# A layer norm + linear attention + gelu MLP block on one core: stages over all tokens instead of an interleaved schedule

## The chip, the cores and the metric

One core of a Trainium2 chip. The metric is the device time of one execution in microseconds (us); smaller is better. Most executions agree within about 1.5%. Now and then one execution has a much lower granted TensorE clock (0.757 in a run of 331.8 us for the kernel before); such slow runs are listed apart and no reading below uses them. PE is TensorE, DVE is VectorE, ACT is ScalarE, POOL is GpSimd.

## The reference, cut to what matters

```python
# x: (1, 2048, 640)   32 heads of width 20   hidden width F = 1536   all bf16
xn = layernorm(x)
q, k, v = split_heads(xn @ wqkv)                # three (2048, 640) matrices
phi(t)  = where(t > 0, t + 1, exp(t)) + 1e-6
kv  = sum over tokens of phi(k)^T v             # per head, 20x20
z   = sum over tokens of phi(k)                 # per head, 20
o   = (phi(q) @ kv) / (phi(q) @ z + 1e-6)       # per head
mlp = gelu_tanh(xn @ w1 + b1) @ w2 + b2
return x + o @ wo + mlp
```

## The kernel before

It works in two parts. First, token tile by token tile (16 tiles of 128), it normalises, transposes, computes K and V together and adds phi(K)^T V into PSUM. Then, in four chunks of 512 tokens, it interleaves Q, the MLP's hidden blocks ("h"), the attention division and the output products. The hidden block:

```python
def h_head(c, jb):                                      # one block: 128 hidden columns x 512 tokens
    # ... 5 matmuls of 512 columns into H_ps[s2]
    act(hsh, H_ps, Identity, bias=b1h, scale=0.5)       # ScalarE
    act(sq,  H_ps, Square,   bias=b1h, scale=0.5)       # ScalarE
    dve.tensor_scalar(vv, sq, C1x4, C0, mult, add)      # VectorE
    dve.tensor_tensor(uu, vv, hsh, mult)                # VectorE
    # later units:
    act(th, uu, Tanh, scale=2.0)                        # ScalarE, same table as Exp
    dve.scalar_tensor_tensor(GT, th, 1.0, hsh, add, mult)
# ... (cut)
def g_units(c):                                         # the interleaved order
    us = []
    for t in range(DT):                                 # DT = 5
        us += [("qt", c, t), ("h", c, t), ("h", c, t + DT)]
    us += [("den", c), ("h", c, 2 * DT), ("h", c, 2 * DT + 1), ("rdenT", c)]
    return us
# ... (cut) output: W2 (12 blocks) and Wo (5 blocks) as 512+128 columns per token tile
```

Of the kernel before, what the change touches and what calls it, by code (L numbers as in the profile page):

```python
# [5 lines left out]
ALU = AluOpType  # L6
ACT = mybir.ActivationFunctionType
P = 128
# [104 lines left out]
def bass_parallel_sum__linear_attn_block__dense_activation_gelu__prompt_kernel(  # L113
# [3 lines left out]
    assert Batch == 1 and D % P == 0 and F % P == 0 and S % 512 == 0  # L117
# [8 lines left out]
    assert DH * H == D  # L126
# [4 lines left out]

    with contextlib.ExitStack() as es:
        sb = lambda *a, **k: es.enter_context(nc.sbuf_tensor(*a, **k))

        x_res = sb("x_res", [P, NT, D], BF16)
        xnT = sb("xnT", [P, DT, S], BF16)
        Wkv = sb("Wkv", [P, DT, 2 * D], BF16)
        Wq = sb("Wq", [P, DT, D], BF16)
        W1 = sb("W1", [P, DT, F], BF16)
        Wo = sb("Wo", [P, DT, D], BF16)  # L140
        W2 = sb("W2", [P, JT, D], BF16)
        b1tmp = sb("b1tmp", [JT, P], BF16)
        b1h = sb("b1h", [P, JT], FP32)
        b2bc = sb("b2bc", [P, D], BF16)
        ones_row = sb("ones_row", [1, P], BF16)
        ones_col = sb("ones_col", [P, 1], BF16)
        ident = sb("ident", [P, P], BF16)
        stats = sb("stats", [P, 3, 12], FP32)
        aggr = sb("aggr", [P, 3, 2], FP32)
        rstd = sb("rstd", [P, 3], FP32)  # L150
        nmr = sb("nmr", [P, 3], FP32)
        veps = sb("veps", [P, 3], FP32)
        epscol = sb("epscol", [P, 1], FP32)
        mhalf = sb("mhalf", [P, 1], FP32)
        xn_tm = sb("xn_tm", [P, 2, D], BF16)
        ek = sb("ek", [P, 2, D], BF16)
        rk = sb("rk", [P, 2, D], BF16)
        PK = sb("PK", [P, 2, D], BF16)
        Vaug = sb("Vaug", [P, 2, D + DT], BF16)

        e0 = [DH * ((P * dt) // DH) for dt in range(DT)]
        e1 = [DH * (-((-(P * (dt + 1))) // DH)) for dt in range(DT)]
        Wd = [e1[dt] - e0[dt] for dt in range(DT)]
        voff = []
        acc = 0
        for dt in range(DT):
            voff.append(acc)
            acc += Wd[dt] + 1
        VAW = acc
        Vaug = sb("Vaug2", [P, 2, VAW], BF16)  # L170
        maskKV = [sb(f"maskKV{dt}", [P, Wd[dt]], BF16) for dt in range(DT)]
        mt_lo = [e0[dt] // P for dt in range(DT)]
        mt_hi = [(e1[dt] - 1) // P for dt in range(DT)]
        kvw_base = [mt_lo[dt] * P for dt in range(DT)]
        kvw_w = [(mt_hi[dt] - mt_lo[dt] + 1) * P for dt in range(DT)]
        KVW = [sb(f"KVW{dt}", [P, kvw_w[dt]], BF16) for dt in range(DT)]
        pairs = [[dt for dt in range(DT) if mt_lo[dt] <= mt <= mt_hi[dt]] for mt in range(DT)]
        EB = sb("EB", [P, DT, H], BF16)
        ZB = sb("ZB", [P, DT, H], BF16)
        z_sb = sb("z_sb", [P, DT], FP32)  # L180
        E32 = sb("E32", [H, D], BF16)
        PQT = sb("PQT", [P, 2, DT, CW], BF16)
        eqb = sb("eqb", [P, 4, CW], BF16)
        rq = sb("rq", [P, 4, CW], BF16)
        den_sb = sb("den_sb", [P, CH, H], FP32)
        rden = sb("rden", [P, CH, H], BF16)
        rdenT = sb("rdenT", [H, CW], BF16)
        numsb = sb("numsb", [P, 4, CW], BF16)
        OT = sb("OT", [P, 2, DT, CW], BF16)
        hsh = sb("hsh", [P, 4, CW], BF16)  # L190
        sq = sb("sq", [P, 4, CW], BF16)
        vv = sb("vv", [P, 4, CW], BF16)
        uu = sb("uu", [P, 4, CW], BF16)
        th = sb("th", [P, 4, CW], BF16)
        GT = sb("GT", [P, 2, JT, CW], BF16)
        out_sb = sb("out_sb", [P, 2, D], BF16)

        ps = es.enter_context(nc.psum_tensor("ps", [P, 8 * 512], FP32))

# [3 lines left out]
        def bankbf(b, lo=0, hi=1024):  # L203
            return ps[:, b * 512:(b + 1) * 512].bitcast(BF16)[:, lo:hi]

        psT = [bankbf(6, 0, DT * P), bankbf(7, 0, DT * P)]
        K_A = bank(2, 0, 512)
        K_B = bank(3, 0, D - 512)
        K_full = ps[:, 2 * 512: 2 * 512 + D]
        V_A = bank(4, 0, 512)  # L210
        V_B = bank(5, 0, D - 512)
        V_full = ps[:, 4 * 512: 4 * 512 + D]
        KVB0, KVB1 = 0, 1
        kvb = {}
        order6 = [0, 1, 3]
        order7 = [2, 4]
        off = 0
        for dt in order6:
            kvb[dt] = (KVB0, off)
            off += Wd[dt] + 1  # L220
        assert off <= 512
        off = 0
        for dt in order7:
            kvb[dt] = (KVB1, off)
            off += Wd[dt] + 1
        assert off <= 512

        def kv_block(dt, extra=True):
            b, o = kvb[dt]
            return bank(b, o, o + Wd[dt] + (1 if extra else 0))  # L230

        b1T_ps = bankbf(2, 0, JT)

        qT_ps = [bank(4), bank(5)]
        H_ps = [bank(6), bank(7)]
        NUM_ps = [bank(0), bank(2)]
        R_ps = [bank(1), bank(3)]
        NUM_psl = [bank(4), bank(6)]
        R_psl = [bank(5), bank(7)]
        FA = [bank(0), bank(2)]  # L240
        FB = [bank(1, 0, D - 512), bank(3, 0, D - 512)]
        F_full = [ps[:, 0:D], ps[:, 2 * 512: 2 * 512 + D]]

        r_x = [R_("x%d" % c) for c in range(NC)]
        r_xnT = [R_("xnT%d" % t) for t in range(NT)]
        r_Wkv, r_Wq, r_W1, r_Wo, r_W2 = R_("Wkv"), R_("Wq"), R_("W1"), R_("Wo"), R_("W2")
        r_b1tmp, r_b1h, r_b2bc = R_("b1tmp"), R_("b1h"), R_("b2bc")
        r_xt = [R_("xt%d" % t) for t in range(NT)]
        r_identc = R_("identc")
        r_csmall = R_("csmall")  # L250
        r_mask = R_("mask")
        r_EB, r_E32 = R_("EB"), R_("E32")
        r_stats = [R_("stats%d" % i) for i in range(3)]
        r_aggr = [R_("aggr%d" % i) for i in range(3)]
        r_rstd = [R_("rstd%d" % i) for i in range(3)]
        r_nmr = [R_("nmr%d" % i) for i in range(3)]
        r_veps = [R_("veps%d" % i) for i in range(3)]
        r_xn = [R_("xn0"), R_("xn1")]
        B_ = [R_("bank%d" % i) for i in range(8)]
        r_psT = [[B_[6]], [B_[7]]]  # L260
        r_K, r_V = [B_[2], B_[3]], [B_[4], B_[5]]
        r_ek = [R_("ek0"), R_("ek1")]
        r_rk = [R_("rk0"), R_("rk1")]
        r_PK = [R_("PK0"), R_("PK1")]
        r_Va = [R_("Va0"), R_("Va1")]
        r_KV = [B_[0], B_[1]]
        r_KVW = R_("KVW")
        r_zsb, r_ZB = R_("zsb"), R_("ZB")
        r_b1T = [B_[2]]
        r_qT = [[B_[4]], [B_[5]]]  # L270
        r_eq = [R_("eq%d" % i) for i in range(4)]
        r_rq = [R_("rq%d" % i) for i in range(4)]
        r_PQT = [R_("PQT0"), R_("PQT1")]
        r_den, r_densb, r_rden, r_rdenTps, r_rdenT = [B_[5]], R_("densb"), R_("rden"), [B_[5]], R_("rdenT")
        r_H = [[B_[6]], [B_[7]]]
        r_NUM = [[B_[0]], [B_[2]]]
        r_R = [[B_[1]], [B_[3]]]
        r_NUMl = [[B_[4]], [B_[6]]]
        r_Rl = [[B_[5]], [B_[7]]]
        r_numsb = [R_("numsb%d" % i) for i in range(4)]  # L280
        r_OT = [[R_("OT%d_%d" % (c_, m_)) for m_ in range(DT)] for c_ in range(2)]
        r_hsh = [R_("hsh%d" % i) for i in range(4)]
        r_sq = [R_("sq%d" % i) for i in range(4)]
        r_vv = [R_("vv%d" % i) for i in range(4)]
        r_uu = [R_("uu%d" % i) for i in range(4)]
        r_th = [R_("th%d" % i) for i in range(4)]
        r_GT = [[R_("GT%d_%d" % (c_, j_)) for j_ in range(JT)] for c_ in range(2)]
        r_F = [[B_[0], B_[1]], [B_[2], B_[3]]]
        r_out = [R_("out0"), R_("out1")]

        xv = A_x.rearrange("b s d -> (b s) d")

        def dma_x(c):
            srcx = xv[c * CW:(c + 1) * CW, :].rearrange("(t p) d -> p t d", p=P)
            Pl.ins("sync", lambda e: e.dma_start(x_res[:, c * CH:(c + 1) * CH, :], srcx),
                   writes=[r_x[c]], dma=True)

        dma_x(0)
        Pl.ins("scalar", lambda e: e.dma_start(
            Wkv[:], A_wqkv[:, D:3 * D].rearrange("(kt p) n -> p kt n", p=P)), writes=[r_Wkv], dma=True)  # L300
        Pl.ins("sync", lambda e: e.dma_start(b1tmp[:], B_b1.rearrange("(a p) -> a p", p=P)),
               writes=[r_b1tmp], dma=True)
        Pl.ins("sync", lambda e: e.dma_start(b2bc[:], B_b2.rearrange("(a d) -> a d", a=1).partition_broadcast(P).rearrange("p a d -> p (a d)")),
               writes=[r_b2bc], dma=True)
        for c in range(1, NC):
            dma_x(c)
# [19 lines left out]
        for s_ in range(2):  # L326
            Pl.ins(g, lambda e, s_=s_: e.memset(Vaug[:, s_, :], 1.0), writes=[r_Va[s_]])
# [34 lines left out]
        def run_mask_jobs(n):  # L362
            for _ in range(n):
                job = next(mj_iter, None)
                if job is None:
                    return
# [439 lines left out]
```

## Time and profile before

| | before |
|---|---|
| time, median of 4 runs | 284.52 us (283.24 to 286.00) |
| span of the profiled execution | 281.2 us |
| PE busy / not busy | 233.7 / 47.5 us |
| mean granted clock | 0.975 |

The page of the kernel before: busy time by engine, then PE's busy tenths and the granted clock in 40 slices of 7.0 us.

```profile
span 281.2 us, 4108 instructions
...
PE 233.7 (83%) x1504; PEld 118.1 (42%) x1533; DVE 170.7 (61%) x360; ACT 154.8 (55%) x297; POOL 53.9 (19%) x98
...
PE   0389988888788348979997979999797999979785
...
PEclk9999999999999969999999999999889999979999
```

No engine is full. PE is the busiest and has a hole at the start, another a third of the way through (digits 3 and 4, from 91 to 105 us), and many slices of 7 or 8.

The timeline of PE in the K/V stage: start, duration, instruction.

```profile
60.33 0.22 PE L426 MATMUL ps<-Wkv,xnT 128*128 128x128 bf16 x1
60.39 0.38 PE L424 MATMUL ps<-Wkv,xnT 128*128 128x512 bf16 x1
60.60 0.22 PE L426 MATMUL ps<-Wkv,xnT 128*128 128x128 bf16 x1
60.66 0.38 PE L424 MATMUL ps<-Wkv,xnT 128*128 128x512 bf16 x1
```

Read the starts, not the durations: a 512-column matmul starts at 60.39, the next at 60.66. So 640 columns pass in 0.27 us, 2.37 per ns, although a single matmul is recorded as 0.38 us long; matmuls are pipelined, and the weight load of each (98 ns) is hidden too. Counting the kernel's columns (about 513,600) gives an estimate of 217 us of streaming as the floor of this schedule.

Groups of instructions of the hidden blocks: busy us and mean ns of one, then the engine's idle time before them.

```profile
L584 ACT ACTIVATE hsh<-ps,b1h 128x512 bf16<-128x512 f32 x48 | 32.8, 683 | 36.0 <-PE ps L579 36.0
L598 ACT ACTIVATE th<-uu 128x512 bf16<-128x512 bf16 x48 | 30.4, 634 | 21.5 <-DVE uu L593 21.4
...
L587 ACT ACTIVATE sq<-ps,b1h 128x512 bf16<-128x512 f32 x48 | 32.8, 684 | 0.0
```

Each hidden block costs ScalarE about 2 us (three passes of 0.63 to 0.68), while PE needs 1.08 us for it. The trace has one table load, of 1283 ns, for the Exp and the Tanh together.

The stretches of the kernel before: bounds, length, busy time of each engine (instructions in brackets), then the granted clock and the DMA share.

```profile
0.00:12.20 12.20, 0.93 (x7) 0.58 (x8) 2.45 (x8) 1.28 (x1) 3.21 (x14) 1.00 0.83 271
12.20:75.30 63.10, 55.83 (x468) 34.22 (x477) 45.59 (x106) 45.21 (x112) 50.70 (x84) 1.00 0.30 107
75.30:102.50 27.20, 16.61 (x74) 6.84 (x73) 20.98 (x54) 19.90 (x35) 0.00 (x0) 0.95 0.00 0
102.50:255.00 152.50, 139.94 (x832) 66.71 (x848) 94.91 (x185) 85.41 (x144) 0.00 (x0) 0.96 0.04 14
255.00:281.20 26.20, 20.36 (x127) 9.79 (x129) 6.74 (x9) 2.99 (x5) 0.00 (x0) 0.99 0.07 26
```

The columns are PE, weight loads, DVE, ACT, POOL. The third line is the first chunk of Q and hidden blocks, where there is no output product yet to fill PE: PE is busy 16.6 of 27.2 us.

### The profile page before, as it was taken

To read this page: it belongs to the slowest core of one execution; us is meant where nothing else is said; L and a number is where in the kernel's file an instruction comes from. 1 tells how busy PE (TensorE), PEld (TensorE's weight loads), DVE (VectorE), ACT (ScalarE), POOL (GpSimd) and SP (SyncE) were. 2 spreads that over 40 slices of the span, in tenths; PEclk is the share of its full clock that TensorE was granted. 3 is DMA by queue.
4 is the path that set the end of the run, shared out by engine and by line. 5 is a ranking of instruction groups with operands and counts; after the bars stand their busy time and mean duration, and the time that the engine had idled before them with its cause. 6 is when DMAs were issued, how large, how long until landed. Compare 5 with 4: busy or idle time off the path is not lost.

```text
span 281.2 us, 4108 instructions
## 1 busy us (share of the span) xinstructions
PE 233.7 (83%) x1504; PEld 118.1 (42%) x1533; DVE 170.7 (61%) x360; ACT 154.8 (55%) x297; POOL 53.9 (19%) x98
## 2 busy tenths in 40 slices
PE   0389988888788348979997979999797999979785
PEld 0255555555433123345553325555233555534242
DVE  0567787778278886754557885346958544580512
ACT  1077777787598807843347883534867344560300
POOL 3188898899000000000000000000000000000000
PEclk9999999999999969999999999999889999979999
DMA  7999200000000000000000000000000001000011
GB/s 250 318 382 372 103 5 0 2 0 0 2 0 0 0 3 1 0 0 26 23 23 26 0 0 2 23 24 30 20 0 0 25 9 38 26 0 0 8 41 47
DMA packets 8780, 12.87 MB, mean 46 GB/s; under 512 B 441, under 2 KB 7481, under 8 KB 8761
## 3 DMA queue, kind: packets, MB, share of 16 engines
q1 hardware_dynamic: 8104, 10.98, 11.2%
q10 hardware_dynamic: 656, 1.64, 1.6%
q8 instruction: 12, 0.20, 0.3%
q14 instruction: 8, 0.06, 0.1%
HBM read 10.00 MB, written 2.62 MB: 45 GB/s over the span
## 4 chain that ended last, share of the span: by engine, by line
PE 67%; DVE 16%; ACT 9%; issue 5%; DMA 2%; POOL 0%; SPq 0%; ACTq 0%; DVEq 0%
PE ps L671 15%; PE ps L579 11%; PE ps L416 6%; PE ps L550 6%; PE ps L687 6%; PE ps L424 5%; PE ps L673 5%; PE ps L651 4%; ACT sq L587 3%; DVE xnT L407 3%; DVE uu L593 2%; DMA b1tmp<-in_B_b_dram 2%; PE ps L401 2%; PE ps L644 2%; PE ps L418 2%
## 5 line engine op out<-in xcount | busy, mean ns | idle before, releaser
L579 PE MATMUL ps<-xnT,W 128*128 128x512 bf16 x232 | 59.2, 390 | 3.7 <-ACT sq L587 3.3
L671 PE MATMUL ps<-W,GT 128*128 128x512 bf16 x182 | 53.9, 388 | 6.2 <-ACT th L598 4.3
L584 ACT ACTIVATE hsh<-ps,b1h 128x512 bf16<-128x512 f32 x48 | 32.8, 683 | 36.0 <-PE ps L579 36.0
L673 PE MATMUL ps<-W,GT 128*128 128x128 bf16 x192 | 42.6, 222 | 0.5
L598 ACT ACTIVATE th<-uu 128x512 bf16<-128x512 bf16 x48 | 30.4, 634 | 21.5 <-DVE uu L593 21.4
L590 DVE TENSOR_SCALAR vv<-sq 128x512 bf16<-128x512 bf16 x48 | 13.8, 288 | 45.1 <-ACT sq L587 45.1
L579 PEld LDWEIGHTS ps<-xnT,W 128*128 128x128 bf16 x240 | 22.7, 100 | 32.0 <-ACT sq L587 6.1
L604 DVE SCALAR_TENSOR_TENSOR GT<-th,hsh 128x512 bf16<-128x512 bf16 x48 | 32.4, 683 | 0.9
L587 ACT ACTIVATE sq<-ps,b1h 128x512 bf16<-128x512 f32 x48 | 32.8, 684 | 0.0
L671 PEld LDWEIGHTS ps<-W,GT 128*128 128x128 bf16 x192 | 19.1, 99 | 31.4 <-ACT th L598 3.8
L416 PE MATMUL ps<-Wkv,xnT 128*128 128x512 bf16 x73 | 22.8, 396 | 3.3 <-DVE xnT L407 3.3
L550 PE MATMUL ps<-xnT,Wq 128*128 128x512 bf16 x99 | 25.1, 385 | 0.2 <-issue 0.2
L432 ACT ACTIVATE ek<-ps 128x640 bf16<-128x640 f32 x16 | 11.3, 705 | 24.9 <-PE ps L418 24.9
L451 ACT ACTIVATE Vaug<-ps 128x140 bf16<-128x140 f32 (+1 forms) x80 | 23.5, 293 | 2.0
L687 PE MATMUL ps<-Wo,OT 128*128 128x512 bf16 x78 | 23.1, 379 | 0.3 <-DVE OT L659 0.3
L424 PE MATMUL ps<-Wkv,xnT 128*128 128x512 bf16 x79 | 23.2, 379 | 0.0
L438 POOL TENSOR_TENSOR x_res<-x_res,b2bc 128x640 bf16<-128x640 bf16 x16 | 22.9, 1432 | 0.6 <-DVE xn_tm L393 0.6
L559 DVE TENSOR_SCALAR rq<-ps 128x512 bf16<-128x512 f32 x20 | 13.7, 686 | 13.4 <-ACT eqb L555 13.3
L593 DVE TENSOR_TENSOR uu<-vv,hsh 128x512 bf16<-128x512 bf16 x48 | 20.4, 426 | 1.6
L418 PE MATMUL ps<-Wkv,xnT 128*128 128x128 bf16 x80 | 17.9, 224 | 3.0 <-DVE xnT L407 2.9
L695 DVE TENSOR_TENSOR out_sb<-ps,x_res 128x640 bf16<-128x640 f32 x16 | 13.1, 820 | 10.8 <-PE ps L689 10.8
L673 PEld LDWEIGHTS ps<-W,GT 128*128 128x128 bf16 x192 | 19.1, 99 | 1.2
(66 smaller groups left out, 314.0 us busy)
## 6 DMA issues: line engine op xcount, KB each, us to landing
W<-in_B_w_dram SPq DMA_DIRECT2D x2, 1920.0 KB, 16.5
x_res<-in_A_x_dram SPq DMA_DIRECT2D x4, 640.0 KB, 11.0
out_dram<-out_sb SPq DMA_DIRECT2D x16, 160.0 KB, 1.8
Wkv<-in_A_wqkv_dram ACTq DMA_DIRECT2D x1, 1600.0 KB, 10.5
Wq<-in_A_wqkv_dram SPq DMA_DIRECT2D x1, 800.0 KB, 13.5
Wo<-in_A_wo_dram SPq DMA_DIRECT2D x1, 800.0 KB, 14.4
b2bc<-in_B_b_dram SPq DMA_DIRECT2D x1, 160.0 KB, 8.2
b1tmp<-in_B_b_dram SPq DMA_DIRECT2D x1, 3.0 KB
```

The source lines that it names most:

```text
L416: fns.append(lambda e, kt=kt, lhsT=lhsT: e.matmul(K_A, lhsT, Wkv[:, kt, 0:512], start=(kt == 0), stop=(kt == DT - 1)))
L424: fns.append(lambda e, kt=kt, lhsT=lhsT: e.matmul(V_A, lhsT, Wkv[:, kt, D:D + 512], start=(kt == 0), stop=(kt == DT - 1)))
L550: fns.append(lambda e, kt=kt: e.matmul(qT_ps[s2], Wq[:, kt, dt * P:(dt + 1) * P], xnT[:, kt, cc], start=(kt == 0), stop=(kt == DT - 1)))
L579: fns.append(lambda e, kt=kt: e.matmul(H_ps[s2], W1[:, kt, jb * P:(jb + 1) * P], xnT[:, kt, cc], start=(kt == 0), stop=(kt == DT - 1)))
L584: Pl.ins("scalar", lambda e: e.activation(hsh[:, s4, :], H_ps[s2], ACT.Identity, bias=b1h[:, jb:jb + 1], scale=0.5), reads=r_H[s2] + [r_b1 ...
L587: Pl.ins("scalar", lambda e: e.activation(sq[:, s4, :], H_ps[s2], ACT.Square, bias=b1h[:, jb:jb + 1], scale=0.5), reads=r_H[s2] + [r_b1h], ...
L593: Pl.ins("vector", lambda e: e.tensor_tensor(out=uu[:, s4, :], in0=vv[:, s4, :], in1=hsh[:, s4, :], op=ALU.mult), reads=[r_vv[s4], r_hsh[s ...
L598: Pl.ins("scalar", lambda e: e.activation(th[:, s4, :], uu[:, s4, :], ACT.Tanh, scale=2.0), reads=[r_uu[s4]], writes=[r_th[s4]])
L604: Pl.ins("vector", lambda e: e.scalar_tensor_tensor(out=GT[:, cs, jb, :], in0=th[:, s4, :], scalar=1.0, in1=hsh[:, s4, :], op0=ALU.add, op ...
L671: (lambda e, jb=jb, lhsT=lhsT: e.matmul(FA[fs], lhsT, W2[:, jb, 0:512], start=(jb == 0), stop=False)),
L673: (lambda e, jb=jb, lhsT=lhsT: e.matmul(FB[fs], lhsT, W2[:, jb, 512:D], start=(jb == 0), stop=False)),
L687: (lambda e, et=et, lhsT=lhsT: e.matmul(FA[fs], lhsT, Wo[:, et, 0:512], start=False, stop=(et == DT - 1))),
```

## The change

The intent: run each kind of work over all 2048 tokens before the next, so that the gelu table is loaded once and each hidden block needs one ScalarE pass; drop V (G = xn^T phi(K), 640x640, is computed instead, and Wv^T G masked per head gives KV); take Q's columns with stride 5, so that each 128-row block holds four rows of every head and one matmul gives the denominators already broadcast; fold KV and Wo into one 640x640 matrix M; and accumulate MLP output and attention output in one PSUM pair, split 320+320. The core of the diff, heavily cut:

```diff
@@ hidden blocks: all tokens first, narrow segments at the start @@
-            Pl.ins("scalar", ... hsh ... ACT.Identity ...)     # and sq, th on ScalarE,
-            Pl.ins("vector", ... vv ...)                       # vv, uu, GT on VectorE
+            Pl.ins("scalar", lambda e: e.activation(
+                HG[:, jb, tok], bank(b, 0, w), ACT.Gelu_apprx_tanh, bias=b1c[:, jb:jb + 1]), ...)
+        Pl.ins("tensor", [... bank(wb), warm[:, 0:P], warm[:] ... for _ in range(14)], ...)   # warm-up
+        segs = [(0, 1), (1, 1), (2, 2)] + [(c * CH, CH) for c in range(1, NC)]
+            if si == 1:
+                const_masks()                                   # GpSimd builds the head masks
@@ K, and its sum over tokens on GpSimd @@
+        for t in range(NT):
+            ... K matmuls, exp on ScalarE, min/add and max/add on VectorE -> PK[:, t, :]
+            Pl.ins(g, ... zsum[:] += PK[:, t, :] ...)
@@ G in place of V @@
+        for f in range(DT):
+            ... 16 tiles x 2 halves: xn_tm[:, t, f*P:(f+1)*P], PK[:, t, h*HW:(h+1)*HW]
+            Pl.ins("tensor", fns, reads=r_xn + r_PK, writes=B_[b:b + 2])
@@ Q strided by 5, M, fused output sums @@
+                    bank(b), Wqkv[:, k, j:D:DT], xnT[:, k, cc], ...
+                            bank(b + h, 0, HW), KVT[:, t, j:D:DT], Wo[:, t, h * HW:(h + 1) * HW], ...
+            seq  = [(HG[:, jb, tok], W2[:, jb, :], ...) for jb in range(JT)]
+            seq += [(PQ[:, j, tok], Msb[:, j, :], ...) for j in range(DT)]
```

## The prediction

> **What bounds the kernel now.** TensorE, imperfectly fed. The timeline shows pairs of 512+128-column matmuls every 0.27 us and five 512-column ones every 1.08 us, about 2.37 columns/ns with weight loads (98 ns each) hidden. I count 513,600 columns, so 217 us of streaming in a span of 281. The other 64 us, by the stage windows and the wait list:
> - 12.2 us before the first real matmul (the bias load lands at 7.5 us, VectorE waits behind it, then layernorm);
> - K/V stage, 12.2 to 75.3: about 52 us of streaming in 63, short waits for the xnT copy;
> - 75.3 to 102.5: PE busy 16.6 of 27.2; ScalarE and VectorE (six passes per hidden block, 3.3 us, against 1.08 on PE) set the pace, with one 7.3 us wait for ZB;
> - later, reciprocal and eviction waits and a granted clock of 0.83 to 0.91 in some 20-us windows (mean 0.975).
>
> **What the change does.**
> Columns: V plus KV-accumulation (62,500) becomes G = xn^T phi(K) plus KVT (54,700); numerator, broadcast and output projection (88,000) become M plus its application (67,200); the denominator grows to 10,240; warm-up adds 7,200 in otherwise idle time. About 490,600 without the warm-up, 207 us: only 10 us less. Splitting 640 as 320+320 gains nothing: the 128-column half already streamed at rate.
> Elementwise: one gelu pass (about 0.68 us) replaces the six, removing the first-chunk shortage. It adds a table load (1.28 us), hidden by eight rotating banks.
> So the gain is mostly filled gaps.
>
> **Stages estimated from these durations.**
> - First H matmul at about 9 us.
> - H plus transposes: 56 us streaming plus about 6 us stalls: the first narrow tiles outrun layernorm (2.1 us of VectorE per tile), and the masks, about 5 us on GpSimd (0.21+2x0.34 us each), sit ahead of rstd. Ends near 71.
> - K: 21.6 us on PE, but per tile VectorE needs about 0.35+0.83 us and GpSimd a 1.4 us sum. [...] the two-input PK operation goes from 777 to 1315 ns, the x_res add from 1386 to 1982, at worst. If it holds fully, K paces at about 1.75 us per tile rather than 1.35. G needs every PK tile, so this is exposed: I take 28 us including the last phi.
> - G: 21.6 us; the x_res adds run under it.
> - Q 21.6, z and KVT 2, M 6.8, den 1.1, 1 of stalls: 32.5 us. VectorE needs about 30 us here (reciprocal on 512 columns 3.4 us, scaled from 0.95 on 128).
> - Output: 73.5 plus 3.2 us; VectorE has slack. Tail 3 us.
> Sum about 232.5; measured time exceeds the span by 4.4 us here: **237 us**. 80% range 227 to 250. Chances: faster 0.96, same 0.03, slower 0.01.
>
> **What would show it.** PE busy above 90%; five-matmul groups still 1.08 us; hardly any wait over 3 us except start, masks (20 to 30 us) and K to G; ScalarE busy near 72 us; K tiles spaced over 1.35 us with VectorE waiting for GpSimd; output tiles every 4.6 us without gaps.
>
> **What would make it wrong.** Stride-5 weight loads (Q, M) longer than the 216 or 135 ns matmul that hides them: [...] before has no strided load, so no run shows it yet. [...] Pauses that lower the clock, or VectorE falling behind in Q and den: 3 to 8 us more.

Passages that told of the hardware what no trace or run of this case shows are cut from the recorded prediction and expectations; the cuts are marked. No term of the sum is cut: it came to about 232.5 us of span, with 28 us for K, and with 4.4 us to 237 us of time. The 1.75 us per tile behind K's term is the author's estimate: 0.35 us of VectorE's min/add plus the 1.4 us of GpSimd's sum, as if the two did not overlap at all, which was not shown. The trace of before shows two-input PK operations of 777 to 1315 ns (median 780) and x_res adds of 1386 to 1982 ns (median 1395). It also shows a pause with a slow clock after it: PE did nothing from 96.43 to 99.84 us, and the clock was 0.50 from there to 106.67 us.

## The result, and the profile after

| | before | change |
|---|---|---|
| time, median of 4 runs | 284.52 us | 242.63 us (242.03 to 243.25) |
| span of the profiled execution | 281.2 us | 241.5 us |
| PE busy / not busy | 233.7 / 47.5 us | 223.6 / 17.9 us |
| mean granted clock | 0.975 | 0.972 |

The ratio is 0.8516 (95% interval 0.847 to 0.856). Ratios here are the mean time of one kernel's fast runs over that of the other's of the same rounds, so not quite the ratio of the medians quoted. The change is right to the reference.

The page of the change, the same lines (slices of 6.0 us):

```profile
span 241.5 us, 3734 instructions
...
PE 223.6 (93%) x1524; PEld 147.2 (61%) x1524; DVE 111.9 (46%) x211; ACT 70.8 (29%) x120; POOL 62.8 (26%) x89
...
PE   7596389999999999389999999999999999999995
...
PEclk9889799999999999959999999999999999999999
```

The span fell by 39.7 us: 29.6 of that is PE time that is no longer idle (47.5 to 17.9) and 10.1 is less busy time, although 6.0 us of warm-up matmuls were added. Two holes are left, near 24 to 30 us and near 96 to 104, and the clock is low just after each (0.78 and 0.56, below).

The two groups of the hidden blocks, on the page of the change:

```profile
L321 PE MATMUL ps<-xnT,W 128*128 128x512 bf16 (+2 forms) x360 | 57.3, 320 | 0.7 <-DVE xnT L313 0.7
...
L325 ACT ACTIVATE HG<-ps,b1c 128x512 bf16<-128x512 f32 (+2 forms) x72 | 37.9, 545 | 31.1 <-PE ps L321 30.5
```

ScalarE spends 37.9 us on all hidden blocks, where it spent 96.0 (32.8+32.8+30.4), and now waits for PE rather than PE for it. The change has two table loads, for gelu and for exp, of 1283 ns each. At the switch the last gelu ends at 77.86 us, the load runs from 77.88 to 79.16 and the first exp starts at 79.17; PE was busy throughout (2.03 us of the 2.03 from 77.17 to 79.20).

The stretches of the change, columns as before: start; hidden blocks; K until the first matmul of G; G; Q with M and the first denominators; output.

```profile
0.00:10.20 10.20, 6.54 (x21) 2.36 (x22) 3.71 (x11) 1.28 (x1) 2.48 (x12) 1.00 0.85 267
10.20:77.20 67.00, 60.38 (x437) 36.55 (x438) 27.56 (x72) 37.27 (x72) 17.70 (x46) 0.95 0.33 110
77.20:103.70 26.50, 21.78 (x160) 15.29 (x158) 21.90 (x32) 13.21 (x18) 19.36 (x14) 0.98 0.00 1
103.70:128.30 24.60, 24.57 (x161) 16.82 (x162) 1.39 (x1) 2.82 (x4) 23.22 (x18) 0.89 0.00 1
128.30:161.60 33.30, 33.06 (x191) 21.56 (x189) 22.54 (x49) 14.40 (x24) 0.00 (x0) 1.00 0.01 1
161.60:241.50 79.90, 77.29 (x559) 54.61 (x559) 34.83 (x48) 1.78 (x3) 0.00 (x0) 1.00 0.09 34
```

From 128 us on PE is full. The lost time is in the first 104 us. The two waits of PE that end the holes, from its timeline (in square brackets: idle time, and who ended it):

```profile
27.89 0.72 PE L309 MATMUL ps<-ident,xn_tm 128*128 128x128 bf16 x5 [4.69 <-DVE xn_tm L302]
...
103.73 1.49 PE L396 MATMUL ps<-PKQ,xn_tm 128*128 128x320 bf16 x5 [4.75 <-DVE PKQ L367]
```

And the stretches just after them; the third figure from the end is the granted clock:

```profile
28.00:34.20 6.20, 5.22 (x42) 4.13 (x42) 3.81 (x11) 2.37 (x5) 1.81 (x5) 0.78 0.43 144
...
104.00:110.00 6.00, 6.00 (x27) 3.42 (x26) 1.15 (x1) 0.00 (x0) 5.95 (x5) 0.56 0.00 0
```

VectorE and GpSimd in the middle of K:

```profile
84.17 0.82 DVE L367 SCALAR_TENSOR_TENSOR PKQ<-ps,ek 128x640 bf16<-128x640 f32 x1
84.91 0.69 DVE L365 TENSOR_SCALAR ek<-ek 128x640 bf16<-128x640 bf16 x1
85.70 0.83 DVE L367 SCALAR_TENSOR_TENSOR PKQ<-ps,ek 128x640 bf16<-128x640 f32 x1
```
```profile
84.02 9.11 POOL L386 TENSOR_TENSOR zsum<-zsum,PKQ 128x640 f32<-128x640 f32 x6
```

One tile takes VectorE 1.53 us (84.17 to 85.70) against 1.36 us on PE, and GpSimd adds with hardly a pause (six adds of 1.40 us in 9.11 us). VectorE's min/add (L365) takes 622 ns here. In Q, with GpSimd idle, it takes 286 ns, though on 512 columns instead of 640, so a part of the difference is width. These two groups and the strided weight loads, from the groups by shape:

```profile
L408 PEld LDWEIGHTS ps<-xnT,Wqkv 128*128 128x128 bf16 x100 | 11.7, 117 | 9.5
...
L365 DVE TENSOR_SCALAR ek<-ek 128x640 bf16<-128x640 bf16 x16 | 10.0, 622 | 18.4 <-ACT ek L364 18.4
...
L365 DVE TENSOR_SCALAR ek<-ek 128x512 bf16<-128x512 bf16 x20 | 5.7, 286 | 24.9 <-ACT ek L364 24.9
```

### The profile page after: what moved, and what is told of

Read it like the earlier page. It is cut to its first block, busy times and chain, and to the rows that moved or that the text cites. A ratio compares the mean times of both kernels' runs of the same rounds, so it can differ in the third digit from the quotient of the medians.

```text
span 241.5 us, 3734 instructions
## 1 busy us (share of the span) xinstructions
PE 223.6 (93%) x1524; PEld 147.2 (61%) x1524; DVE 111.9 (46%) x211; ACT 70.8 (29%) x120; POOL 62.8 (26%) x89
## 3 DMA queue, kind: packets, MB, share of 16 engines
HBM read 10.00 MB, written 2.62 MB: 52 GB/s over the span
## 4 chain that ended last, share of the span: by engine, by line
PE 76%; DVE 16%; POOL 3%; issue 2%; ACT 1%; DVEq 0%
PE ps L488 31%; PE ps L321 20%; PE ps L396 10%; DVE PKQ L367 7%; PE ps L408 4%; DVE ek L365 4%; PE ps L441 3%; PE ps L278 2%; PE ps L309 2%; PE ps L451 2%; DVE rden L456 1%; PE ps L416 1%; POOL maskKV L264 1%; POOL maskKV L268 1%; DVE PKQ L458 1%
## 5 line engine op out<-in xcount | busy, mean ns | idle before, releaser
L321 PE MATMUL ps<-xnT,W 128*128 128x512 bf16 (+2 forms) x360 | 57.3, 320 | 0.7 <-DVE xnT L313 0.7
L488 PE MATMUL ps<-W,HG 128*128 128x320 bf16 x384 | 54.9, 299 | 0.3 <-DVE PKQ L367 0.3
L488 PEld LDWEIGHTS ps<-W,HG 128*128 128x128 bf16 x384 | 37.5, 98 | 15.7 <-issue 0.7
L325 ACT ACTIVATE HG<-ps,b1c 128x512 bf16<-128x512 f32 (+2 forms) x72 | 37.9, 545 | 31.1 <-PE ps L321 30.5
L365 DVE TENSOR_SCALAR ek<-ek 128x512 bf16<-128x512 bf16 (+1 forms) x36 | 15.7, 435 | 43.4 <-ACT ek L364 43.4
L364 ACT ACTIVATE ek<-ps 128x512 bf16<-128x512 f32 (+1 forms) x36 | 23.2, 645 | 25.6 <-PE ps L377 9.3
L396 PE MATMUL ps<-PKQ,xn_tm 128*128 128x320 bf16 x160 | 24.6, 321 | 4.8 <-DVE PKQ L367 4.8
L367 DVE SCALAR_TENSOR_TENSOR PKQ<-ps,ek 128x512 bf16<-128x512 f32 (+1 forms) x36 | 27.0, 751 | 4.2 <-PE ps L408 0.5
L488 PE MATMUL ps<-Msb,PKQ 128*128 128x320 bf16 x160 | 24.5, 299 | 0.0
L396 PEld LDWEIGHTS ps<-PKQ,xn_tm 128*128 128x128 bf16 x160 | 16.6, 104 | 12.8 <-DVE PKQ L367 5.1
L408 PE MATMUL ps<-xnT,Wqkv 128*128 128x512 bf16 x100 | 22.1, 379 | 0.0
L377 PE MATMUL ps<-Wqkv,xnT 128*128 128x320 bf16 x160 | 22.0, 299 | 0.0
```

The costliest lines, as they stand in the source:

```text
L321: Pl.ins("tensor", [(lambda e, k=k: e.matmul(bank(b, 0, w), W1[:, k, jb * P:(jb + 1) * P], xnT[:, k, tok], start=(k == 0), stop=(k == DT - ...
L325: Pl.ins("scalar", lambda e: e.activation(HG[:, jb, tok], bank(b, 0, w), ACT.Gelu_apprx_tanh, bias=b1c[:, jb:jb + 1]), reads=[B_[b], r_b1c ...
L364: Pl.ins("scalar", lambda e: e.activation(e2, src, ACT.Exp), reads=br, writes=[r_ek[s]])
L365: Pl.ins(v, lambda e: e.tensor_scalar(et, et, 1.0, 1e-6, ALU.min, ALU.add), reads=[r_ek[s]], writes=[r_ek[s]])
L367: Pl.ins(v, lambda e: e.scalar_tensor_tensor(out=d2, in0=src, scalar=0.0, in1=e2, op0=ALU.max, op1=ALU.add), reads=br + [r_ek[s]], writes= ...
L377: fns.append(lambda e, k=k, h=h, b=b, t=t: e.matmul(bank(b + h, 0, HW), xnT[:, k, t * P:(t + 1) * P], Wqkv[:, k, D + h * HW:D + (h + 1) * ...
```

## The experiments

Two questions. Where does the gain come from: fewer columns, the split of 640, or the elementwise work that no longer starves PE? And what are the remaining holes: the masks, VectorE's slow min/add in K, the clock? The comparisons below use the ratio to the kernel before in the same rounds; the change stands at 0.8516.

### The masks moved behind the last layer norm (a_masks_late)

```diff
-            if si == 1:
+            if si == len(segs) - 2:
                 const_masks()
```

> Change as given, only the mask building on GpSimd moved from after the second token segment to after the last layernorm. If the masks ahead of rstd caused the hole between 23 and 28 us (PE idle for 4.7 us at its longest) and the cold clock after it (0.78 from 28 to 34 us): the hole closes, the clock stays at 1.00, span 241.5 -> 235 to 236, time 236 to 238. If the narrow first segments are limited by the layernorm chain on VectorE itself (2.1 us a tile): the hole only spreads out over the tiles, at most 2 us are gained, time 240 to 242.

Measured: 238.26 us, ratio 0.8392, so 4.4 us less than the change by the medians and 3.5 by the ratios (0.8392/0.8516 of 242.6). PE's transposes at 24.71 us, and the stretch in which the change had a clock of 0.78:

```profile
24.71 0.45 PE L309 MATMUL ps<-ident,xn_tm 128*128 128x128 bf16 x5 [0.98 <-DVE xn_tm L302]
...
28.00:34.00 6.00, 5.02 (x41) 3.35 (x39) 3.53 (x10) 3.06 (x6) 1.74 (x4) 1.00 0.45 151
```

The 4.69 us wait is gone and the clock from 20 to 34 us is 1.00. What is left there are waits of 0.43 to 0.98 us before most tiles' transposes, each ended by the normalisation. The first theory holds in kind; the time is just above its range of 236 to 238, and part of the hole belongs to the layer norm chain.

### The sums of phi(K) after K (a_zsum_late)

```diff
-            elif t > 1:                       # inside the loop over K tiles
-                Pl.ins(g, ... zsum += PK[:, t, :] ...)
+        Pl.ins(g, ... zsum = PK[:, 0, :] + PK[:, 1, :], reads=[..., r_PK[NT - 1]])
+        for t in range(2, NT):                # after the loop
+            Pl.ins(g, ... zsum += PK[:, t, :] ...)
```

> Change as given, only the GpSimd sums of phi(K) start after the last K tile instead of beside them. Theory [...]: the 640-column min/add in K falls from 622 ns to about 320, the K cycle from 1.53 us to the 1.36 us of PE, the wait of G for the last tile from 4.8 to about 2.2 us, perhaps without the cold clock after it; the x_res adds now fall into Q, so the 512-column min/add there rises from 286 ns towards 500. Net 2 to 5 us less: time 238 to 241. Rival (the min/add is slow by itself at this width[...]): 622 ns stays, K and time unchanged, 242 to 243.

Measured: 244.23 us, ratio 0.8598: about 2 us more than the change, so the forecast gain of 2 to 5 us was missed. (The 95% intervals of the two ratios, 0.854 to 0.866 and 0.847 to 0.856, just overlap: that it is slower is not certain.) The groups of VectorE in this run:

```profile
L365 DVE TENSOR_SCALAR ek<-ek 128x512 bf16<-128x512 bf16 x20 | 10.2, 510 | 22.2 <-ACT ek L364 22.2
...
L421 DVE TENSOR_SCALAR ZB<-bmask,z_sb 128x128 bf16<-128x128 bf16 x5 | 5.7, 1135 | 0.2
L365 DVE TENSOR_SCALAR ek<-ek 128x640 bf16<-128x640 bf16 x16 | 5.2, 326 | 19.6 <-ACT ek L364 18.4
```

The K operation fell from 622 to 326 ns with GpSimd's adds moved away from it, so beside them this operation is slowed. By what mechanism is not shown. But GpSimd's x_res adds now run beside Q, and there the same operation rose from 286 to 510 ns and the five ZB products from 255 to 1135 ns. The stretches of this run around G's start and in Q:

```profile
100.00:105.00 5.00, 4.18 (x31) 3.06 (x32) 1.95 (x2) 0.00 (x0) 4.11 (x3) 1.00 0.03 5
```
```profile
135.00:145.00 10.00, 6.74 (x23) 3.16 (x24) 9.20 (x15) 1.90 (x4) 9.86 (x8) 0.66 0.00 0
```

G began after a wait of 2.29 us and with a full clock; in Q a new wait and a cold clock (0.66) appeared. The slowing followed GpSimd's work from K to Q, and moving it there cost more than it saved in K.

### G waits tile by tile (a_g_tilewaits)

```diff
-            Pl.ins("tensor", fns, reads=r_xn + r_PK, writes=B_[b:b + 2])
+            for t in range(NT):
+                Pl.ins("tensor", fns[2 * t:2 * t + 2], reads=[r_xn[t], r_PK[t]], writes=B_[b:b + 2])
```

> Change as given, only the G matmuls of each token tile wait for that tile of phi(K), not the whole group for all 16. K stays paced by VectorE (622 ns min/add). The 4.8 us wait before G shrinks to under 1 us, since 15 of 16 tiles of the first feature block can run. If that wait also cooled the clock (0.56 from 104 to 110 us, about 2.7 us lost): G goes from 24.6 to about 21.8 us and the time to 235 to 236.5. If the clock dips for another reason (the load of G itself): it stays low in G and only 4 us are gained, 238 to 239.

Measured: 237.36 us, ratio 0.8344, 5 us less than the change. Around the start of G:

```profile
97.00:110.00 13.00, 12.67 (x92) 8.57 (x91) 7.89 (x10) 3.12 (x5) 12.28 (x10) 1.00 0.00 1
```

PE is busy 12.67 of 13 us and the clock is 1.00, so the dip of 0.56 in the change was caused by the wait before G, not by G's load. The gain lies between the two forecasts in time; the clock decides for the first. The rest went to Q: G ends 6.5 us earlier than in the change (121.6 against 128.2), but GpSimd's x_res adds now reach into Q, where the 512-column min/add takes 475 ns instead of 286 and Q lasts 1 us longer.

### The bias copied after the first normalisation (a_b1_late)

```diff
-        Pl.ins(v, ... b1c <- transposed bias ...)
-        ln_stats(1)
         ln_norm(0)
         transp(0)
+        Pl.ins(v, ... b1c <- transposed bias ...)
+        ln_stats(1)
```

> Change as given, only VectorE normalises tile 0 before it copies the bias (which waits behind the 14 warm-up matmuls). First H matmul at 8.2 to 8.6 us instead of 10.2, now held by the warm-up on PE itself. If the clock of the first segment (0.54 from 10.2 to 13.9 us) is cold because PE paused from 7.3 to 10.2, it is warm now: another 1.5 us. Time 239 to 241. Rival: the start is set by the W1 load, then nothing changes, 242 to 243.

Measured: 242.70 us, ratio 0.8532: nothing gained. The first hidden matmul did come at 7.53 us instead of 10.18. Then, in PE's timeline:

```profile
14.31 2.94 PE L321 MATMUL ps<-xnT,W 128*128 128x128 bf16 x35 [2.27 <-DMA W<-in_B_w_dram]
...
28.69 0.45 PE L309 MATMUL ps<-ident,xn_tm 128*128 128x128 bf16 x5 [4.70 <-DVE xn_tm L302]
```

PE met the load of W1, which had not landed, and ran at half clock from 15.4 to 18.8 us. The masks on GpSimd then began at 20.47 us instead of 19.68, and the same mask hole ended at 28.69 (27.89 in the change). A gain ahead of a wait that ends at a fixed time is worth nothing. Neither theory as written holds: the first matmul was not held by W1, but what it gained was lost again at W1 and at the masks.

### One gelu pass in the kernel before (b_gelu), and one tanh pass (b_tanh_onepass)

```diff
-            Pl.ins("scalar", ... hsh ...)      # hsh, sq, th on ScalarE; vv, uu, GT on VectorE
-            ...
+            Pl.ins("scalar", lambda e: e.activation(
+                GT[:, cs, jb, :], H_ps[s2], ACT.Gelu_apprx_tanh, bias=b1h[:, jb:jb + 1]), ...)
-                       b1h = 0.5 * b1
+                       b1h = 1.0 * b1
```

The second kernel has `ACT.Tanh` in the same place and gives a wrong result.

> The kernel before, only its gelu: one ScalarE pass with the gelu table in place of three ScalarE and three VectorE passes; the order of the units is left interleaved (Q's exp between the hidden blocks). Theory: one pass alone would help, but exp and gelu now alternate, so the table (1.28 us a load) is changed about twice for each of the 20 Q blocks, some 40 loads or 51 us of ScalarE. That eats the gain: 275 to 290 us (before 284). Rival: ScalarE has so much room that the loads cost nothing: 262 to 270 us, as in the next run.

> Wrong result on purpose: as the run before, but the one pass is tanh, which the trace shows to share a table with exp. It shows what the fewer elementwise passes are worth in the old order without table changes. The first chunk (75 to 102 us in the profile of before, PE busy 16.6 of 27.2 us) becomes bound by PE, later waits for sq, th and GT go: 262 to 270 us, so 15 to 20 of the 42 us that the change gains. Rival (the gain is mainly the fewer columns and the new stages): less than 8 us, 276 to 284.

Measured: tanh 262.98 us, ratio 0.9216; gelu 269.4 us in the median of its three fast runs (269.93 with the slow one), ratio of the fast runs 0.9455. The first execution of the gelu kernel was slow (411.95 us at a clock of 0.571); it happens to be the profiled one (the clock digit of its page is 5 in 38 of the 40 slices, with PE busy 95% of the span), so only its instruction counts and the length of its table loads are used here:

```profile
L584 ACT ACT_TABLE_LOAD x20 | 25.7, 1283 | 0.4
L555 ACT ACT_TABLE_LOAD x19 | 24.4, 1283 | 0.3
```

Dropping the elementwise passes alone is worth about 21 us in the old order: half of the 42 us, and just more than the 15 to 20 forecast. The 39 table loads, 50.1 us of ScalarE, cost about 7 us of time, far less than I expected. The forecast of 275 to 290 us was missed and the time lies in the rival's range, although the loads are not free. With the three passes gone ScalarE has room (in the tanh run it is busy 103.3 us of 261.4), so most loads probably pass beside PE's work; that is not shown, since the only trace is the slow run's. So the separation into stages is not what makes one gelu pass affordable. The first-chunk stretch of the tanh run:

```profile
75.30:102.50 27.20, 22.86 (x117) 10.14 (x118) 11.79 (x28) 11.61 (x19) 0.00 (x0) 0.87 0.00 1
```

PE is busy 22.9 us there where it was 16.6.

### The split 512+128 kept (a_split512)

```diff
+    SP = [(0, 512), (512, D)]
-                        bank(b + h, 0, HW), xn_tm[...], PK[:, t, h * HW:(h + 1) * HW], ...
+                        bank(b + h, 0, SP[h][1] - SP[h][0]), xn_tm[...], PK[:, t, SP[h][0]:SP[h][1]], ...
     # the same in K, M and the output products
```

> Change as given, only the 640-column products split 512+128 as before instead of 320+320 (K, G, M, output). Prediction on record: the split gains nothing, since the traces show both streaming at about 2.37 columns/ns with weight loads hidden. Time within 1% of the change, 241 to 244. If the short 128-column matmul exposed its weight load (98 ns), 377 pairs would lose about 40 ns each: 15 us, 255 to 258.

Measured: 243.28 us, ratio 0.8538. No difference from the change. The prediction's statement holds.

### No warm-up (a_nowarm)

```diff
-        Pl.ins("tensor", [... bank(wb), warm[:, 0:P], warm[:] ... for _ in range(14)], ...)
```

> Change as given, without the 14 warm-up matmuls. In the profile of the change they hold up the bias transpose behind them until 7.1 us, and the clock is cold again (0.54) when the first segment runs. So they buy nothing: first H matmul near 7.5 instead of 10.2, later waits (last W1 quarter near 14 us, the masks until 27 us) take that back; 241.5 to 243.5, within 0.5% of the change. If they do warm something, 2 us more: 244.5 to 246.

Measured: 242.95 us, ratio 0.8531: the same time, as expected. In PE's timeline:

```profile
9.96 3.36 PE L319 MATMUL ps<-xnT,W 128*128 128x128 bf16 x30 [0.68 <-DVE xnT L311]
```

The first hidden matmul came at 9.96 us and not at 7.5: without the warm-up the bias lands at 5.40 us, and VectorE still does the bias and a second tile's statistics before the first normalisation. In the change the 14 matmuls end at 7.2 us, PE then does little until 10.2, and the first segment runs at a clock of 0.54 (10.2 to 13.9 us; 0.50 for the 3.41 us from 10.28). The warm-up buys nothing there.

The clock that the views print for the first microseconds is not a measurement: the packed trace of the change has no clock entry before 6.87 us of the span, that of before none before 14.51, and the views give 1.00 there. In the change the 14 matmuls of 512 columns took 5.96 us, 426 ns each, which is half the later pace (216 ns at 2.37 columns per ns). Here the 30 matmuls at 9.96 us took 3.36 us, where they take 1.83 us in e_pipelined.

### All repairs together (c_all)

Masks behind the layer norms, x_res adds during the hidden blocks, sums of phi(K) under G, G waiting tile by tile, bias copied later, z after the second Q chunk.

> Change with all repairs: masks and x_res adds on GpSimd during the later hidden segments, sums of phi(K) after the K tiles (under G), G waiting tile by tile, bias copied after the first normalisation, z after the second Q chunk. If the found causes add up (start 2.5, masks 4 to 6, K to G and its cold clock 7[...]), the span is about 220 to 224 and the time 222 to 226. If they overlap (a gap closed early is only met later, as the bias copy alone showed): 229 to 234.

Measured: 232.92 us, ratio 0.8168, correct. The repairs do not add up fully. The second half does: G takes 21.73 us at full clock and K ends without a hole. G in the chain that ended last (start, duration):

```profile
96.82 21.73 PE ps L408 x160
```

In the first half, the last quarter of W1 is the new wait, and the clock is cold after it. From the list of waits, and the stretch after:

```profile
PE ps L321 <- DMA W<-in_B_w_dram: 2.5, 1, 2.5
```
```profile
14.00:20.00 6.00, 5.26 (x50) 5.26 (x51) 0.77 (x2) 2.81 (x8) 0.16 (x1) 0.50 1.07 364
```

### W1 loaded ahead of later tiles (d_dma_order), also without warm-up (d_nowarm)

```diff
         for i in range(NW1):
-            dma_w("scalar", W1 quarter i)      # its own queue, beside everything else
+            dma_w("sync", W1 quarter i)        # one queue, in order: x0, W1_0, b1, x1, W1_1, W1_2, W1_3, x2-3, ...
```

> As the run with all repairs, only the four W1 loads go to the same queue as the rest, ahead of the token tiles that are needed later. Theory: the early start was lost because the last W1 quarter, sharing the transfer rate with later loads, landed at 14.7 us and PE, paused, ran cold (0.50 from 14 to 20 us). With W1 there by about 10 us the hidden stage ends near 68 instead of 75 us: span 224 to 226, time 225.5 to 228 (all repairs: 232.9). Rival: the layernorm chain of the first eight tiles (2.1 us each or more on VectorE) is the limit and W1 only hides it: gain under 2.5 us, 230.5 to 233.

> As the run with reordered loads, without the 14 warm-up matmuls. If the warm-up pays there (PE goes straight from it into the hidden stage), the first segment runs at half clock for about 3.4 us and 1.5 to 3 us are lost. If the layernorm chain limits the first segments anyway, the slower matmuls hide in its waits: within 1 us.

Measured: 233.85 us, ratio 0.8212, and without warm-up 234.17 us, ratio 0.8219. Both are the same as all repairs within the intervals. The theory that W1 alone held the start falls. The wait for W1 is gone, but token tiles 2 and 3, now behind it, land at 12 us; VectorE's timeline:

```profile
12.12 0.50 DVE L289 BATCH_NORM_STATS2 stats<-x_res 128x6 f32<-128x320 bf16 x1 [3.65 <-DMA x_res<-in_A_x_dram]
```

The transfer rate is 353 to 364 GB/s through this time, so the 2.62 MB of W1 and the first four tiles, 7.3 us at that rate by estimate, cannot all be there much earlier; the order only chooses what waits. After that the tiles come 2.52 us apart, one layer norm after another.

### Statistics between normalisation and copy (e_pipelined)

```diff
             if i == 1:
+                dma_x(2, 2)                     # tiles 2 and 3 ahead of the second half of W1
 ...
-                    ln_stats(nst); ln_norm(t); transpose(t); copy(t)
+                    ln_norm(t); transpose(t); ln_stats(nst); copy(t)
```

> The run with reordered loads (layernorm tiles 2 to 8 came 2.52 us apart there, since VectorE waits about 0.55 us for each tile's own transposes before it copies them, and the first three tiles arrived behind W1), with two edits: VectorE does the next tile's statistics between a tile's normalisation and its copy, and token tiles 2 and 3 are loaded ahead of the second half of W1. If the layernorm chain limits the first 33 us: tiles come about 2.0 us apart, PE is dense from about 27 us, the hidden stage ends near 68 to 70 instead of 75 us, span 224 to 227, time 226 to 229 (run before 233.9). Rival: the transfer rate (about 360 GB/s until 28 us) or ScalarE in the narrow segments limits: under 2 us gained, 232 to 234.

Measured: 230.37 us, ratio 0.8085, correct. This is the best version here, 5% under the change and 3.5 us under the run that it was built from; it lies between the two forecasts (226 to 229 and 232 to 234). But the mechanism is not the one expected. The normalisations in VectorE's timeline:

```profile
13.04 0.45 DVE L304 TENSOR_SCALAR xn_tm<-x_res,aggr,rstd 128x640 bf16<-128x640 bf16 x1 [0.72 <-POOL rstd L298]
...
15.73 0.45 DVE L304 TENSOR_SCALAR xn_tm<-x_res,aggr,rstd 128x640 bf16<-128x640 bf16 x1 [0.72 <-POOL rstd L298]
```

The tiles are 2.69 us apart, not 2.0: the wait for the transposes was traded for a wait of 0.72 us for GpSimd's rstd, since the statistics now come just before the normalisation that needs them. What improved is that no wait at the start was long (1.15 us at most after the first hidden matmul) and the clock stayed at 1.00 in every stretch, 0.999 in the mean. The hidden stage ends at 72.1 us (75.1 with all repairs, 77.2 in the change). The load order and the edit of the chain were made together, so how much each gave is not separated.

## Why the prediction was right or wrong

The measured 242.63 us lies in the stated range of 227 to 250, 5.6 above the 237 forecast. Stage by stage, in us of the span:

| step | forecast | measured | shown by |
|---|---|---|---|
| first hidden matmul | 9 | 10.2 | profile |
| hidden stage ends | 71 | 77.2 | profile, a_masks_late |
| K until G | 28 | 26.5 | profile, a_zsum_late |
| G | 21.6 | 24.6 | a_g_tilewaits, c_all |
| Q, M, first denominators | 32.5 | 33.3 | profile |
| output and tail | 79.7 | 79.9 | profile |
| sum | 232.5 as stated (the terms give 232.8) | 241.5 | |
| time minus span | 4.4 | 1.7 | |

- **PE bounds the kernel, imperfectly fed, and the gain is mostly filled gaps: right.** PE's idle time fell by 29.6 us of the 39.7. The tanh run gains 21 us with no column removed. "Splitting 640 as 320+320 gains nothing" is shown by a_split512.
- **The hidden stage was mis-sized, by 5 us.** The term was "56 us streaming plus about 6 us stalls"; the stage took 67.0 us. PE was idle for 6.6 us of it, so the stalls were sized well, but it was busy for 60.4 us and not 56. What was left out is the clock: PE was busy for 6.3 us in two stretches at half clock, which lost about 3 us (an estimate from these figures). The masks were named as a cause, rightly: moving them gains about 4 us, the hole and the slow clock after it (0.78) together. The slow first segment (0.54) cost little. In a_zsum_late, where the start is the same, it ran at full clock (30 matmuls in 1.83 us, not 3.29), and the mask hole still ended at 27.40 us against 27.89.
- **"Warm-up adds 7,200 in otherwise idle time": the time was idle, but VectorE waited for the bias transpose queued behind it**, and the clock was cold again (0.54) when real work came. Taking it out changes nothing (a_nowarm, d_nowarm).
- **VectorE's min/add slowed beside GpSimd in K: right in kind, its size overestimated.** The pace was 1.53 us, not the 1.75 I added up from both engines' durations, an estimate; the operation rose from 326 ns alone (a_zsum_late) to 622. The forecast of 28 us for K became 26.5.
- **G was mis-sized by 3 us**, and the cause is shown: 21.6 us holds at full clock (21.73 in c_all), and the change ran G at 0.89 since it came after a wait of 4.75 us. The prediction listed "pauses that lower the clock" as a way to be wrong but priced none, though it forecast the pause itself. Where PE was dense before the wait, 4.75 us lowered the clock (0.56) and 2.29 us in a_zsum_late did not (1.00). At the thinly busy start a wait of 2.5 us was enough (c_all, 0.50).

The packed traces show the pattern behind both. They record the clock in slots of 3.41 us, and the clock of a slot goes with PE's busy time in the slot before. In the 13 profiled executions that were not slow, all 25 full-clock slots with less than 1.40 us of PE work were followed by half clock, and all 821 with more than 1.55 us by full clock (four slots in between went either way). All 10 half-clock slots with at most 2.55 us were followed by half clock again, and all 24 with at least 2.75 us by full clock. In the change PE did nothing from 99.03 to 102.44 us, so the next slot ran at half clock; PE was busy for 2.12 us of that one, so the third did too. Half of 2.12 + 3.41 is 2.8 us, and that is what G lost (24.57 against 21.73). In c_all the slot from 10.25 to 13.66 us held 1.29 us of work. In e_pipelined no slot before the tail held less than 1.72, and the clock never fell. This was read from the records; no run was made to test it.

- **Stride-5 weight loads: the feared cost did not come.** They took 117 ns instead of 98, hidden under the matmuls (PE was busy 33.06 of the 33.30 us of that stage); the 50 matmuls of M took 6.8 us, the forecast.
- **Two errors cancelled.** I took 4.4 us as the difference of time and span, by subtracting the profiled span from a median of other executions. In the profiled execution of the change it is 1.75 us (243.25 less 241.5), and that execution was 0.6 us above the median. The span was underestimated by 9.0 us, the time only by 5.6: that part of the agreement is luck.

What stays open: how the other half of the gain, about 21 us, divides. By the column count about 10 us of it are fewer columns, an estimate; the replacement of V, the strided Q, the fused output sums and the order of stages were never run alone. Open too is how the 3.5 us that e_pipelined gains on d_dma_order divide between load order and chain.

## What to carry to other kernels

Estimate a pause of the matrix engine as two costs, the wait and the slow clock after it (here half clock after any 3.41 us slot with less than about 1.4 us of work), and give a consumer's waits the grain of its producer (one tile, not sixteen): here that alone gave 5 us. Before moving work to a less used engine, ask which engine it slows there (here a min/add from 326 to 622 ns) and where the work will run instead, since the slowing moved along with it (286 to 510 ns in Q). And a gain ahead of a wait that ends at a fixed time (a load, a mask) is worth nothing until that wait is moved too.
